# Packed attention and a routed expert layer on one core: token scores computed transposed and turned back, under a new written order

## Chip, core and metric

The kernel runs on one core of one Trainium2 chip. The metric is device time in microseconds: 563.17 us is the median of three runs of the kernel before (560.61 to 563.75). The profiled execution took 564.29 us, of which 562.5 us lie between the first and the last instruction.

## What is computed

Two attentions in a row, for 8 batches and 8 heads with 64 values each, and then a layer of eight experts in which each token goes to one.

```python
p_packed = sm_attn(p, k, v)          # 32 packed queries, 576 keys
out = sm_attn(q, p_packed, p_packed) # 576 tokens, 32 packed keys
x = out.transpose(0, 2, 1, 3).reshape(4608, 512)
e = argmax(x @ w_gate)               # one expert per token
result = gate * (relu(x @ w1[e]) @ w2[e])
```

The token scores that this case is about are q times the packed keys, in the second attention: for each token, 8 heads times 32 scores.

## The kernel before

Everything that happens up to the end of the first layer of the first phase of the experts stands in a list, `ORDER` (line 51). A token of it is one step of one generator: `S20` is the next step of the scores of batch 2, tokens 0 to 255; `c4` the next step of the scores of packed queries of batch 4, second half of the heads. `emit` (line 1051) runs one step per token, and the instructions go to their engines in that order, under `tc.manual_schedule()`. So the list is the order on every queue: TensorE (PE), VectorE (DVE), ScalarE (ACT), GpSimd (POOL), and the DMA queue of SyncE (SP). Waits between the engines are added from the tiles that instructions read and write; `need` and `acquire` only assert, while the program is built, that the list respects what they name.

The letters that matter here:

- `k`, `v`, `q` load a batch's keys with its packed queries (line 585), values (602) and tokens in two halves and a rest (610), all on SP. `cst` loads constants, the identity among them (979).
- `a` and `c` (`s1`, 630) are the scores of the packed queries: per step two matmuls with 64 stationary columns each, which stand side by side in the array, 288 columns moving (648), then a maximum on DVE and an exponential on ACT. There is one PSUM tile for them, so a `c` waits for the exponential of the `a` ahead of it.
- `r`, `u`, `l` (`tr`, `trl`, 686 and 701) turn the result by transposes, `p` (`pv`, 717) multiplies by the values, `b` (`bd`, 756) and `w` (771) prepare the packed keys (`ppT`, two heads side by side: 128 by 64) and values for the second attention.
- `S` (`s2`, 793) makes the token scores. For 256 tokens (second index 0 or 2) it has the q tile as stationary operand, 128 tokens at a time, and 64 columns of `ppT` moving: eight float32 matmuls (803). Each shows as two records in the trace. The result lies in a PSUM tile `s2` (two of them), a row per token. Then come a maximum (829), a subtraction (834), an exponential (838), a sum (842) and a product on POOL or, from batch 6 on, DVE (848). With index 4 it takes the last 64 tokens of two batches (816).
- `T` (`t2`, 854) transposes the probabilities, and `O` (`o2`, 870) multiplies them by the packed values (898, 900) and copies the result on ACT (905).
- The first 14 result tiles of `O` are held in the space of the second layer's weights (`spare`, 785) until a `W` step writes them out (787).
- `L` loads a weight block, `C` (`convert_w`, 933) splits one into two float16 parts with one ACT and one DVE instruction; `C8` to `C15` are of the second layer and write where held tiles lay.
- `R`, `E`, `F` route tokens (many small DVE steps), `G` gathers rows, `P` (538) transposes them, `M` (1212) is the first expert layer.

`tr` is a ring of four PSUM tiles that `r`, `u`, `l`, `p`, `b`, `w`, `T`, `O` and some routing steps share.

The step that changes, in the kernel before:

```python
T.matmul(
    ps[:, 256 * n + 64 * pr : 256 * n + 64 * pr + 64],
    loaded[b]["q"][i // 2][:, pr, P * n : P * n + P],
    ppTs[b % HB][:, pr, :],
    start=True,
    stop=True,
)
```

After the list come the remaining phases of the experts (from line 1238 on), whose order the builder's scheduler sets.

Of the kernel before, what the change touches and what calls it, by code (L numbers as in the profile page):

```python
# [8 lines left out]
F32 = mybir.dt.float32  # L9
# [7 lines left out]
P = 128  # L17
# [39 lines left out]
S14 S14 S12 S12 S12 T10 O00 O02 S20 r3 q2 k5 S22 v3 T10 O10 l4 S20 T12 S14 O10 k6 O10 T12 l4 l4 S20 S20 a5 c3 a5 O10
C0 O10 O02 L2 a5 O10 O12 O10 C0 O12 u4 u4 O10 O12 a5 c4 L3 w2 T14 O10 S22 c5 O12 w2 S20 O12 c5 O12 I k6 T14 O14 S22
q3 c5 r4 C1 O14 O12 C1 O14 p3 r4 p3 p3 p3 q3 S22 q3 c5 l5 O14 c5 O12 v4 O12 b3 S20 k7 l5 O00 a6 C2 u5 a6 L4 c4 b3
S32 l5 T20 S32 S30 S22 C3 O14 r5 a6 O10 S22 O12 R R R R R R R R R T20 R S32 R q4 S30 R R u5 O20 T22 a6 c6 O20 r5 S32  # L60
L5 S30 S34 T22 c6 O20 O20 C2 R O20 S34 c6 O20 O22 p4 k7 R p4 S32 S32 S30 O20 p4 C4 q4 O22 O22 p4 R O20 b4 O22 S32 w3
# [5 lines left out]
O42 S50 O40 O40 q6 E O42 E S52 E E S52 b6 T50 b6 c7 S52 E c7 E E u7 O42 L7 L8 T50 S54 S62 E l7 S62 S52 O50 S60 E O42
E S62 O40 E q7 l7 E u7 O50 S54 C6 O50 S60 O40 E O50 L9 O50 O50 l7 O40 O40 O50 O50 O40 S62 q7 O50 w6 r7 E E E E E O40
E S60 E S52 E S60 E w6 C7 E O50 E T54 W2 W3 O50 E S62 S62 T52 T54 r7 E E O54 O50 O54 S60 C7 O54 O54 p7 p7 T52 O52 E
S60 E p7 E O54 E O52 W4 W5 W6 W7 O52 O54 O52 W8 b7 p7 Z O52 W9 b7 O52 S60 q7 S62 O52 O52 O52 Z T62 O52 T62 O52 T60  # L70
S72 C6 O52 F S72 F F X F X T60 F X F F F O62 O62 F F F O62 S72 F F F F O62 W10 S72 W11 W12 W13 O62 F O62 O62 X S72
O62 F F O62 O60 F O62 L10 F S72 F F X O60 F O60 O60 S70 O62 S74 S72 O62 F X w7 T72 C8 T72 F S74 F F w7 S70 O72 O72
O72 O60 O72 F S74 O60 S74 F G0 S70 F S70 F S74 F O72 O60 F L11 S74 F X O72 S70 O60 F O60 F S70 O72 O60 O72 F O72 O72
T74 T74 S70 P0 F P0 G1 G2 P1 P1 P0 P2 F O60 P1 F F O74 P2 T70 F F F T70 F P2 O74 O74 O60 F G3 P3 P3 F O74 O72 F F
O72 F G4 O70 G5 O70 O70 C9 O70 F C10 C8 L12 F F P3 F F O70 F O70 F O70 O70 F O70 G6 G7 G8 C9 O74 F O70 F F F F O70 F
F C11 C12 O70 C11 O74 Y V0 M0 M0 M1 P4 P5 M0 P4 P5 M1 M2 M2 P4 M0 P5 M3 P6 V1 M0 C10 P6 P6 M1 M3 M4 M2 M3 M4 P7 P8
# [38 lines left out]
def packed_attention_moe(ctx, tc, qT, q1, kT, v4, v1, pT, wg, w1, w2, const, out):  # L115
# [442 lines left out]
    if True:  # L558
# [234 lines left out]
        def s2(b, i):  # L793

            need(f"b{b}", *([f"b{b - 1}"] if i == 4 else []))
            need(*([f"q{b}", f"q{b - 1}"] if i == 4 else [f"q{b}{i // 2}"]))
            acquire("s2", 2, f"s2free{b}{i}")
            ps = psq.tile([P, 512], F32, tag="s2", name="s2")
            if i < 4:
                hh = 2 * H  # L800
                for n in range(2):
                    for pr in range(NP):
                        T.matmul(  # L803
                            ps[:, 256 * n + 64 * pr : 256 * n + 64 * pr + 64],
                            loaded[b]["q"][i // 2][:, pr, P * n : P * n + P],
                            ppTs[b % HB][:, pr, :],
                            start=True,
                            stop=True,
                        )
                    if n == 0:  # L810
                        yield
            else:
                hh = H
                for pr in range(NP):
# [9 lines left out]
            done.add(f"s{b}{i}")  # L824
# [26 lines left out]
            done.add(f"e1free{b}{i}")  # L851
            es[b, i] = e
# [580 lines left out]
```

## Time and profile before

| | us |
|---|---|
| median of three runs | 563.17 (560.61 to 563.75) |
| the profiled execution | 564.29 |
| its span, first to last instruction | 562.5 |
| busy in the span: PE / DVE / ACT / POOL | 537.1 / 451.3 / 324.4 / 194.4 |
| first and last token-score matmul of 256 tokens starts (line 803) | 24.2 / 133.9 |
| first matmul of the first expert layer starts (line 1097) | 147.4 |

A busy time is the union of the records of an engine. Matmuls are pipelined, so a record is longer than the distance to the next start; where a duration decides, the distance of two starts is read. The granted clock is the share of TensorE's full 2.4 GHz.

### The profile page before, as it was taken

The page shows a single profiled execution, that of the slowest core. Times are in us where ns is not written, and L with a number is a line of the kernel's source. Part 1 is how long each engine was busy: PE and PEld are TensorE (multiplying, and loading weights), DVE is VectorE, ACT ScalarE, POOL GpSimd, SP SyncE. Part 2 cuts the span into 40 slices and gives each one's busy share as a digit, 9 for nine tenths or more (in the row PEclk, how much of TensorE's full clock was granted, in tenths as well). Part 3 has the DMA queues.
Part 4 walks back from the last instruction along what each step waited for, and adds up shares of the span by engine and source line. Part 5 has one row for each costly group of instructions (what it writes and reads, how often), then busy time and mean ns, then how long its engine had stood idle before and what let it go on. Part 6 is the DMA issues. An engine that isn't in the chain of part 4 may idle for free.

```text
span 562.5 us, 13282 instructions
## 1 busy us (share of the span) xinstructions
PE 537.1 (95%) x4055; PEld 322.8 (57%) x4055; DVE 451.3 (80%) x928; ACT 324.4 (58%) x663; POOL 194.4 (35%) x277
## 2 busy tenths in 40 slices
PE   4999999998898999999999999999999999999994
PEld 2687687876565456544644655565456456545541
DVE  1366788989998989998999797777449998997962
ACT  2355866566786877734853762366868438736600
POOL 3122333225661102400210266477823302302374
PEclk9999999998999999999999999999999999999998
DMA  8899866999897956984996599378869968975883
GB/s 315 333 399 386 323 247 195 356 325 314 285 223 181 273 185 158 282 196 172 267 244 235 151 170 342 109 169 188 298 252 255 267 212 174 293 255 143 184 239 125
DMA packets 118615, 136.71 MB, mean 243 GB/s; under 512 B 82895, under 2 KB 95311, under 8 KB 116624
## 3 DMA queue, kind: packets, MB, share of 16 engines
q1 hardware_dynamic: 112624, 116.65, 71.8%
q0 software_dynamic: 5920, 19.14, 10.6%
q8 instruction: 41, 0.67, 0.5%
q14 instruction: 30, 0.25, 0.1%
HBM read 97.49 MB, written 19.14 MB: 207 GB/s over the span
## 4 chain that ended last, share of the span: by engine, by line
PE 80%; DVE 10%; ACT 3%; issue 3%; DMA 2%; POOL 0%; POOLq 0%; SPq 0%; DVEq 0%; ACTq 0%
PE py L1156 30%; PE psa L1097 19%; PE psa L1100 9%; PE s L803 5%; PE x L898 5%; PE s L648 4%; PE psx L544 2%; PE pv L739 2%; DVE y L1165 1%; DVE w1r L188 1%; PE t L864 1%; PE tr L695 1%; DVE u L1106 1%; DMA h<-hs 1%; ACT a L663 1%
## 5 line engine op out<-in xcount | busy, mean ns | idle before, releaser
L1097 PE MATMUL psa<-w1r,x 128*128 (+1 forms) x656 | 194.4, 380 | 1.6 <-DVE w1r L188 1.1
L1156 PE MATMUL py<-w2r,h 128*128 (+1 forms) x984 | 195.6, 379 | 0.0
L1100 PE MATMUL psa<-w1r,x 128*128 (+1 forms) x656 | 161.6, 273 | 0.0
L1156 PEld LDWEIGHTS <-h 128*128 128x128 f16 (+1 forms) x984 | 87.5, 100 | 101.6 <-issue 2.9
L1123 POOL TENSOR_TENSOR hs<-u,hs 128x256 f16<-128x256 f32 x74 | 64.7, 876 | 221.2 <-DVE hs L1120 203.7
L1097 PEld LDWEIGHTS <-x 128*128 128x128 f16 (+1 forms) x656 | 58.8, 100 | 68.0 <-issue 2.4
L1165 DVE SCALAR_TENSOR_TENSOR y<-py,gpl,y 128x512 f32<-128x512 f32 x111 | 79.8, 739 | 13.6 <-PE py L1156 13.5
L1104 ACT ACTIVATE u<-psa 128x256 f32<-128x256 f32 x148 | 52.6, 376 | 42.2 <-PE psa L1100 38.2
L188 DVE SCALAR_TENSOR_TENSOR w1r<-stage,w1r 128x1024 f16<-128x1024 f32 x48 | 58.8, 1225 | 11.7 <-ACT w1r L187 11.7
L188 DVE SCALAR_TENSOR_TENSOR w2r<-stage,w2r 128x1024 f16<-128x1024 f32 x48 | 59.8, 1246 | 10.2 <-ACT w2r L187 10.1
L187 ACT ACTIVATE w1r<-stage 128x1024 f16<-128x1024 f32 x48 | 49.2, 1048 | 27.9 <-DMA stage<-w 27.9
L1100 PEld LDWEIGHTS <-x 128*128 128x128 f16 (+1 forms) x656 | 58.9, 100 | 8.6 <-issue 2.4
L1106 DVE SCALAR_TENSOR_TENSOR u<-psa,u 128x256 f32<-128x256 f32 x148 | 57.5, 412 | 7.6 <-ACT u L1104 7.3
L187 ACT ACTIVATE w2r<-stage 128x1024 f16<-128x1024 f32 x48 | 50.2, 1045 | 1.1 <-DMA stage<-w 1.1
L1127 DVE SCALAR_TENSOR_TENSOR hs<-u,hs 128x256 f16<-128x256 f32 x74 | 39.8, 539 | 6.1 <-ACT hs L1125 5.8
L1176 POOL DMA_INDIRECT out_rows<-y,sca x37 | 38.6, 1044 | 12.8 <-issue 8.6
L1125 ACT ACTIVATE hs<-u 128x256 f16<-128x256 f32 x74 | 30.4, 412 | 21.2 <-DVE u L1106 18.4
L1118 ACT ACTIVATE u<-u 128x256 f32<-128x256 f32 x74 | 30.6, 414 | 19.0 <-DVE u L1106 19.0
L547 ACT ACTIVATE x<-psx,xup 128x512 f16<-128x512 f32 x37 | 25.0, 686 | 26.5 <-PE psx L544 26.4
L898 PE MATMUL x<-bd,a2T 128*128 128x264 f32 x128 | 37.3, 418 | 0.0
L549 DVE SCALAR_TENSOR_TENSOR x<-psx,xup,x 128x512 f16<-128x512 f32 x37 | 27.4, 746 | 5.9 <-ACT x L547 5.8
L803 PEld LDWEIGHTS s<-ppT,q 128*128 128x128 f32 x256 | 30.8, 192 | 2.0 <-issue 0.9
(180 smaller groups left out, 633.5 us busy)
## 6 DMA issues: line engine op xcount, KB each, us to landing
stage<-w SPq DMA_DIRECT2D x112, 512.0 KB, 4.6
v<-v SPq DMA_DIRECT2D x8, 1024.0 KB, 10.3
q<-qT SPq DMA_DIRECT2D x16, 512.0 KB, 8.8
k<-kT SPq DMA_DIRECT2D x7, 1152.0 KB, 6.3
xd<-x SPq DMA_DIRECT2D x22, 256.0 KB, 5.2
xd<-w2r SPq DMA_DIRECT2D x14, 256.0 KB, 4.6
h<-hs SPq DMA_TRANSPOSE x76, 4.6
k<-kT SPq DMA_DIRECT2D x2, 576.0 KB, 5.1
```

The source lines that it names most:

```text
L187: A.activation(hi, src, AF.Copy, scale=SW)
L188: V.scalar_tensor_tensor(lo, src, SW, hi, op0=ALU.mult, op1=ALU.subtract)
L803: T.matmul(ps[:, 256 * n + 64 * pr : 256 * n + 64 * pr + 64], loaded[b]["q"][i // 2][:, pr, P * n : P * n + P], ppTs[b % HB][:, pr, :], st ...
L898: T.matmul(ps, aT[:, 2 * n + g, :], bds[b % HB][:, g, :], start=True, stop=True)
L1097: T.matmul(ps[c], x[:, 0, k, c], w, start=(k == 0), stop=False, **kw)
L1100: last["T"] = T.matmul(ps[c, 0:FC], x[:, 1, k, c], w, start=False, stop=(k == 3), **kw)
L1104: A.activation(u, ps[:, FC:], AF.Copy, scale=SH)
L1106: V.scalar_tensor_tensor(u, ps[:, 0:FC], SH, u, op0=ALU.mult, op1=ALU.add)
L1123: last["G"] = G.tensor_tensor(hs[:, 1], u, hs[:, 0], op=ALU.subtract)
L1127: last["V"] = V.scalar_tensor_tensor(hs[:, 1], u, 0.0, hs[:, 0], op0=ALU.max, op1=ALU.subtract)
L1156: last["T"] = T.matmul(ps[c], h[:, hp, f, c], w, start=(n == 0), stop=(n == 5), **kw)
L1165: last["V"] = V.scalar_tensor_tensor(y, ps, at(gpls, j), y, op0=ALU.mult, op1=ALU.add)
```

## The change

1. `s2` for 256 tokens: the packed keys are now the stationary operand (64 columns, two side by side at partitions 0 and 64) and 256 tokens of q move. That is two steps of two matmuls, into a tile of the `tr` ring. ACT copies this tile (128 by 512) to a new SBUF tile `sT` (two of them), and four PE transposes turn it back into the `s2` tile. What follows is as before. There are two more steps per unit, and 16 such units.
2. `convert_w` asserts, for a second-layer block, only the held tiles that lie in its own stretch of the space, and not all 14.
3. `ORDER` is written anew: 1074 tokens where there were 1042.

```diff
 ORDER = """
-k0 k0 a0 a0 a0 a0 cst c0 k1 c0 c0 cst c0 r0 r0 k1 v0 c0 l0 c0 k2 a1 l0 k2 a1 u0 q0 a1 l0 a1 c1 c1 u0 p0 c1 p0 p0 r1
-c1 q0 r1 l1 wgs p0 b0 l1 c1 a2 b0 a2 S02 a2 k3 S02 a2 c2 S02 c2 S00 l1 c2 c2 S02 u1 r2 S00 v1 S00 S00 k3 a3 u1 c1
...
-O62 F O62 O62 O60 F O62 L10 F S72 F F X O60 F O60 O60 S70 O62 S74 S72 O62 F X w7 T72 C8 T72 F S74 F F w7 S70 O72 O72
...
+q0 k0 k0 a0 a0 a0 a0 k1 cst v0 cst q0 k1 wgs c0 wgs c0 c0 c0 c0 r0 u0 l0 a1 u0 r0 k2 a1 l0 k2 v1 c0 l0 p0 a1 a1 p0
+c1 p0 c1 b0 c1 I b0 p0 S02 S00 S00 c1 S02 k3 c1 S00 a2 a2 a2 S00 w0 S02 S00 q0 q1 q1 q1 a2 r1 w0 r1 l1 l1 S00 u1 l1
...
+O62 S72 O62 W13 F G0 F C8 C9 O62 O60 O62 S70 T74 T70 F T74 F O62 S72 F X T70 O74 O74 F S72 O74 O74 F O70 F O70 X O74
+F L10 F F O70 F O62 F T72 F O62 X F O70 T72 F O72 P0 F O72 L11 O72 F O74 O70 F F F F G1 F F G2 F G3 O70 F F F P0 P0
...
             if i < 4:
                 hh = 2 * H
-                for n in range(2):
-                    for pr in range(NP):
+                acquire("tr", 4, f"st{b}{i}")
+                pt = pst.tile([P, 2, 256], F32, tag="tr", name="sT")
+                for g in range(2):
+                    for j in range(2):
                         T.matmul(
-                            ps[:, 256 * n + 64 * pr : 256 * n + 64 * pr + 64],
-                            loaded[b]["q"][i // 2][:, pr, P * n : P * n + P],
-                            ppTs[b % HB][:, pr, :],
+                            pt[64 * j : 64 * j + 64, g, :],
+                            ppTs[b % HB][:, 2 * g + j, :],
+                            loaded[b]["q"][i // 2][:, 2 * g + j, :],
                             start=True,
                             stop=True,
                         )
-                    if n == 0:
+                    if g == 0:
                         yield
+                done.add(f"s{b}{i}")
+                yield
+                acquire("sT", 2, f"sT{b}{i}")
+                sT = wk.tile([P, 2, 256], F32, tag="sT", name="sT")
+                A.copy(sT, pt)
+                done.add(f"st{b}{i}")
+                yield
+                acquire("s2", 2, f"s2free{b}{i}")
+                ps = psq.tile([P, 512], F32, tag="s2", name="s2")
+                for n in range(2):
+                    for g in range(2):
+                        T.transpose(ps[:, 256 * n + P * g : 256 * n + P * g + P], sT[:, g, P * n : P * n + P], ident)
+                done.add(f"sT{b}{i}")
...
-            need(f"stage{w}", *([f"x{t}" for t in range(14)] if w[0] else []))
+            need(f"stage{w}", *([f"x{t}" for t in range(ND) if t < (w[2] + 1) * 4096 / 2112 and t + 1 > w[2] * 4096 / 2112] if w[0] else []))
```

## Rows read from the trace of the kernel before

**Rows 1.** The page's busy times and its chain by engine.
```profile
PE 537.1 (95%) x4055; PEld 322.8 (57%) x4055; DVE 451.3 (80%) x928; ACT 324.4 (58%) x663; POOL 194.4 (35%) x277
...
PE 80%; DVE 10%; ACT 3%; issue 3%; DMA 2%; POOL 0%; POOLq 0%; SPq 0%; DVEq 0%; ACTq 0%
```

**Rows 2.** Busy time by stretch: length, PE, PEld, DVE, ACT, POOL, clock, DMA share, GB/s.
```profile
24.00:115.00 91.00, 90.36 (x1152) 71.72 (x1149) 69.12 (x181) 56.50 (x134) 27.41 (x52) 1.00 0.86 319
115.00:148.00 33.00, 28.36 (x301) 22.20 (x301) 30.55 (x111) 20.45 (x47) 15.62 (x19) 0.95 0.94 302
148.00:182.00 34.00, 31.23 (x217) 20.83 (x216) 30.90 (x73) 25.77 (x58) 15.71 (x17) 1.00 0.87 227
182.00:262.00 80.00, 78.93 (x438) 40.70 (x437) 77.37 (x154) 49.87 (x86) 11.69 (x13) 1.00 0.83 221
262.00:562.00 300.00, 292.43 (x1820) 158.99 (x1818) 238.61 (x401) 164.98 (x327) 116.96 (x148) 0.99 0.80 216
```

**Rows 3.** Chain that ended last, in order of time: start us, us, what.
```profile
36.02 2.63 PE s L803 x24
...
39.65 0.84 PE s L803 x8
...
40.48 0.44 PE t L864 x4
...
52.14 1.73 PE s L803 x16
...
74.72 0.49 PE s L648 x4
```

**Rows 4.** Timeline of PE, 36 to 60 us: start us, us, engine, line, operation.
```profile
39.03 0.61 PE L898 MATMUL x<-bd,a2T 128*128 128x264 f32 x2
39.48 1.00 PE L803 MATMUL s<-ppT,q 128*128 128x64 f32 x8
...
48.47 1.06 PE L898 MATMUL x<-bd,a2T 128*128 128x264 f32 x4
49.36 0.60 PE L695 MATMUL tr<-cst,a 128*128 128x128 f32 x4
...
54.75 0.61 PE L898 MATMUL x<-bd,a2T 128*128 128x264 f32 x2
55.29 1.19 PE L648 MATMUL s<-k,pb 128*64 128x288 f32 x8
56.41 1.16 PE L898 MATMUL x<-bd,a2T 128*128 128x264 f32 x4
57.41 0.60 PE L695 MATMUL tr<-cst,a 128*128 128x128 f32 x4
```

**Rows 5.** Groups of ACT, 24 to 115 us: count, busy us, mean ns, idle before.
```profile
L698 ACT COPY aT<-tr 128x512 f32<-128x512 f32 x12 | 7.1, 590 | 1.8 <-PE tr L695 1.8
```

**Rows 6.** DMA rate in 40 slices of the stretch 0 to 60 us.
```profile
GB/s 0 121 350 406 443 412 418 389 275 399 328 287 313 95 326 427 404 382 403 388 423 392 369 388 376 411 435 421 397 421 426 332 270 424 380 405 399 409 423 373
```

**Rows 7.** Timeline of all engines, 0 to 24 us.
```profile
1.17 0.42 SPq L592 DMA_DIRECT2D k<-kT  x1
...
5.18 2.19 PE L648 MATMUL s<-k,pb 128*64 128x288 f32 x8 [5.18 <-DMA k<-kT]
...
11.20 1.12 PE L695 MATMUL tr<-cst,a 128*128 128x128 f32 x4
...
17.31 2.19 PE L648 MATMUL s<-k,pb 128*64 128x288 f32 x8 [0.68 <-ACT a L663]
...
19.43 1.08 PE L739 MATMUL pv<-v,aT 128*32 128x64 f32 x32
```

**Rows 8.** Timeline of PE, 110 to 150 us.
```profile
126.55 3.01 PE L898 MATMUL x<-bd,a2T 128*128 128x264 f32 x12
...
132.69 0.63 PE L864 MATMUL t<-cst,e 128*128 128x128 f32 x4 [1.50 <-DVE n L335]
...
134.05 4.62 PE L898 MATMUL x<-bd,a2T 128*128 128x264 f32 x12
```

**Rows 9.** Busy time by engine in stretches of 5 us (columns as in rows 2).
```profile
135.00:140.00 5.00, 4.76 (x21) 3.72 (x19) 4.23 (x18) 3.90 (x11) 2.22 (x3) 0.75 0.86 304
```

More of the change, by code (lines that the diff above doesn't have):

```diff
@@ L57 @@
[L57 to L61, printed above, removed]
@@ L67 @@
[L67 to L71, printed above, removed]
@@ L72 @@
[L72 to L76, printed above, removed]
@@ new lines @@
+c1 p0 c1 b0 c1 I b0 p0 S02 S00 S00 c1 S02 k3 c1 S00 a2 a2 a2 S00 w0 S02 S00 q0 q1 q1 q1 a2 r1 w0 r1 l1 l1 S00 u1 l1
+c2 S00 u1 c2 c2 c1 k3 S02 S00 c2 k4 p1 p1 u2 a3 u2 S02 p1 a3 S00 b1 T00 b1 p1 S02 w1 k4 S10 a3 a3 S10 c3 S02 q2 T00
+c3 c3 O00 c2 w1 S02 S12 S10 O00 S12 c3 O00 r2 O00 O00 S10 v2 q2 S14 S10 S12 L0 l2 l2 r2 l2 u3 u3 S14 l3 S14 l3 S02
+k5 T02 T02 a4 v3 O00 S10 S10 S14 O02 S10 a4 S14 S10 S12 l3 O02 O00 p2 S12 a4 a4 O00 O02 T10 p2 c4 O02 c4 c2 p2 T10
+O00 O02 I p2 S14 S12 S12 O00 b2 b2 O02 O10 O10 O10 c3 k5 c4 O10 L1 O02 O10 c4 S22 S22 r3 S22 S20 S20 S22 S12 l4 O02
@@ new lines @@
+l4 S20 S22 S20 r3 a5 a5 l4 S22 c4 a5 O10 S12 O02 C0 T12 O10 r4 O10 k6 S20 a5 c5 S20 c5 c5 T12 O10 O12 S20 v4 O02 T14
+r4 O12 k6 T14 S20 O12 w2 w2 O10 q2 O12 q3 q3 S22 O12 c3 O12 O14 O14 O12 u4 c5 q3 O14 p3 p3 u4 O14 C1 S20 O12 a6 S22
+C0 p3 p3 l5 a6 l5 a6 O12 b3 b3 O14 O12 R R T20 C1 R l5 R T20 R R S30 S22 S30 q4 c5 c5 q4 S34 S30 R O20 a6 S34 L2 L3
+L4 S34 T22 O20 c4 S30 O20 T22 O20 S34 R R S30 q4 c6 O20 R O20 c6 R S32 O20 S30 R k7 p4 R S32 S34 S30 C2 S32 S30 C3
+C4 p4 R c6 S32 O22 S34 O22 O22 S30 R O22 p4 b4 p4 C3 R b4 O20 O22 O20 S32 O22 v5 O22 L5 T30 S32 T30 c6 w3 O22 S42
@@ new lines @@
+O22 S42 T34 T34 S42 R S32 w3 O30 O30 O30 O30 O30 O30 O30 C4 S40 k7 R O30 S40 O34 R S40 C2 O30 R O22 r5 R S42 S40 S32
+O30 O34 O34 S42 r5 l6 u5 O34 S42 S32 u5 O34 S42 S40 p5 L6 O30 l6 l6 T32 S40 O20 S42 T32 C5 q5 O34 p5 O32 S40 O32 p5
+q5 a7 O32 O32 C6 p5 w4 C5 q5 a7 b5 O32 q6 b5 O32 a7 O32 S42 O32 w4 c6 W0 O32 O32 S50 O32 S40 S52 C6 S50 T42 O32 a7 E
+E E v6 S54 S54 E T42 S50 E c7 S54 S52 E c7 O42 E S54 L7 S50 S40 c7 S52 O42 O42 E E r6 S50 E c7 q6 u6 S52 O42 E r6 c6
+q6 S50 E T40 E S50 E u6 p6 E p6 T40 O40 E O40 S52 O40 E O40 O42 S54 O42 E p6 W1 E p6 E b6 r7 w5 b6 O42 S62 S62 S50
@@ new lines @@
+r7 O42 w5 E O42 S62 O40 u7 u7 E l7 S54 S52 O42 T54 S62 E S60 l7 S52 S62 c7 S60 O40 E S52 l7 T54 E S50 S60 O40 S62
+O40 O40 E O54 S60 O40 S60 E v7 O40 E c7 T50 S62 O42 S52 E E T50 E O54 O42 q7 O54 p7 O40 S60 p7 T52 E p7 O54 E O50
+S60 C7 q7 W2 E O50 O50 O50 O54 O54 T52 p7 E E b7 C7 E O52 b7 O52 S70 O50 S60 W3 O52 S70 O52 W4 S70 O50 w6 O50 Z O50
+E O50 q7 O52 O50 E S62 E E E L8 E E E O52 w6 S60 S70 E E S74 O52 S62 O52 E O52 E E O50 S74 Z E E T60 W5 W6 O50 S72
+S74 E S70 O52 T60 L9 T62 O52 O52 S74 O60 E T62 O60 O60 E W7 F F F F O60 S74 O60 F S74 F S72 F S72 F F O62 X F S70
@@ new lines @@
+S70 F S72 X F F F O62 F S70 F w7 O62 S72 O62 F W8 W9 F w7 O60 O60 W10 O60 F O60 W11 W12 O60 S72 F X O60 F F X O62
+O62 S72 O62 W13 F G0 F C8 C9 O62 O60 O62 S70 T74 T70 F T74 F O62 S72 F X T70 O74 O74 F S72 O74 O74 F O70 F O70 X O74
+F L10 F F O70 F O62 F T72 F O62 X F O70 T72 F O72 P0 F O72 L11 O72 F O74 O70 F F F F G1 F F G2 F G3 O70 F F F P0 P0
+O72 F O70 P1 O70 F F F P1 O70 F O72 F O72 F O70 G4 F F F P2 P2 P1 O72 O70 O72 C10 O72 F G5 O70 C9 F P2 F P3 P3 G6 P3
+O72 O72 G7 C11 C8 O72 F F L12 Y V0 M0 M0 M1 M1 P4 M0 P5 P4 P5 P4 M0 M2 M2 P6 P5 M2 P6 M1 P6 M2 M3 M3 M1 G8 P7 P8 P7
@@ new lines @@
+C10 M4 P7 P8 G9 P8 V1 P9 M3 M2 C12 P9 M3 M1 M4 G10 M0 P10 G11 G12 G13 G14 P9 P10 P10 M5 M0 P11 P11 M2 M4 P11 C11 M5
+M3 M6 P12 P13 M6 M5 P13 M4 M6 P13 M7 M6 M6 L13 M4 M5 G15 P12 M5 P12 M7 M8 M8 M9 P14 M8 M7 P15 C13 C13 M4 M9 G16 M7
+M1 M8 M8 G17 M10 P14 P14 M9 P15 M10 M11 L14 M7 M3 M6 C12 M9 G18 M8 L15 C14 P15 M11 C15 M11 M12 M9 M10 C15 M12 M13
+P16 P17 M12 M10 M11 P17 P16 P16 M5 M12 M10 M12 P17 M13 M14 M14 M14 M15 M11 P18 P18 M12 M13 M13 P18 M13 M7 M14 C14
+M10 M15 M16 M16 M17 M17 M18 M15 M17 M15 M9 M16 M18 M14 M18 M11 M15 M16 M17 M17 M13 M18 M16 M18 L16 M16 M14 M15 M18
@@ L82 @@
+M17 L17 L18 L19 M18
 """
@@ L796, in s2 @@
             need(*([f"q{b}", f"q{b - 1}"] if i == 4 else [f"q{b}{i // 2}"]))
-            acquire("s2", 2, f"s2free{b}{i}")
-            ps = psq.tile([P, 512], F32, tag="s2", name="s2")
             if i < 4:
                 hh = 2 * H
-                for n in range(2):
-                    for pr in range(NP):
+                acquire("tr", 4, f"st{b}{i}")
+                pt = pst.tile([P, 2, 256], F32, tag="tr", name="sT")
+                for g in range(2):
+                    for j in range(2):
                         T.matmul(
-                            ps[:, 256 * n + 64 * pr : 256 * n + 64 * pr + 64],
-                            loaded[b]["q"][i // 2][:, pr, P * n : P * n + P],
-                            ppTs[b % HB][:, pr, :],
+                            pt[64 * j : 64 * j + 64, g, :],
+                            ppTs[b % HB][:, 2 * g + j, :],
+                            loaded[b]["q"][i // 2][:, 2 * g + j, :],
                             start=True,
@@ L809, in s2 @@
                         )
-                    if n == 0:
+                    if g == 0:
                         yield
+                done.add(f"s{b}{i}")
[11 more added lines that the diff above has]
+                done.add(f"sT{b}{i}")
             else:
                 hh = H
+                acquire("s2", 2, f"s2free{b}{i}")
+                ps = psq.tile([P, 512], F32, tag="s2", name="s2")
                 for pr in range(NP):
@@ L823, in s2 @@
                 ps = ps[:, 0:256]
-            done.add(f"s{b}{i}")
+                done.add(f"s{b}{i}")
             yield
```

13 lines of the change are left out of this document (removed).

## The prediction, made before the changed kernel ran

> **What bounds the kernel now.** The page comes first: PE is busy for 95% of the span, DVE for 80%, ACT for 58%, and the chain that ended last lies on PE for 80% and on ACT for 3% [rows 1]. That is an average, so the busy times by stretch come next [rows 2]. From 24 to 115 us PE is busy 90.36 of 91 us while DVE has 69.12 and ACT 56.50: here the attention is a matter of PE's work, and what PE need not do is gained. From 115 to 182 us PE has 59.6 of 67 us and DVE 61.45: routing, conversions and softmax share DVE, and PE waits now and then. From 182 us on PE is busy 371.4 of 380 us, so a start that is earlier by some time stays earlier by it.
>
> **Token scores, PE's part.** Before, a unit of 256 tokens is 8 float32 matmuls, 16 records. In the chain 24 records take 2.63 us and 8 take 0.84, so one costs 1.79/16 = 0.112 us and a unit 1.79 us; a unit that stands alone took 1.73 [rows 3]. The trace does not show the new form. The nearest rows are the packed queries' scores at line 648: they have the same shape, two 64-column matmuls side by side, with 288 columns instead of 256. Four of their records take 0.49 us [rows 3]; at 256 columns that is 0.436, and for the two steps 0.87. The four transposes that turn the tile back are like those at line 864, 0.44 us for four [rows 3]. New unit: 1.31 us. Over 16 units 16 x (1.79 - 1.31) = 7.7 us less.
>
> Against this stands the change of shape between full and 64-column matmuls. Two records before a line-648 group take 0.54 us (54.75 to 55.29) where two elsewhere take 0.45 (39.03 to 39.48): 0.09. The group itself takes 1.12 (55.29 to 56.41) where two times 0.49 would be 0.98: 0.14. The four records behind it take 1.00 (56.41 to 57.41) where four elsewhere take 0.89 (48.47 to 49.36): 0.11 [rows 3, 4]. One excursion into 64 columns and back thus costs 0.23 to 0.34 us; I take 0.30, nearer the upper end, because what follows is mostly line 898 or transposes. I counted the shapes along both lists, without the routing matmuls: 71 changes before, 107 after, so 18 more excursions, 18 x 0.30 = 5.4 us. PE's net gain is 7.7 - 5.4 = **2.3 us** (1.6 at 0.34, 3.6 at 0.23, 7.7 if excursions were free).
>
> The rows show 0.436 us for a pair of 64-column matmuls and 0.3 us for going there and back. The Trainium skill, TensorEngine Tiling, Performance Considerations, advises just this swap where the moving side has 64 columns or fewer, and its Overview names a speedup of up to 2x; by that alone the sum would be 16 x 0.895 = 14.3 us less for the scores and 7.0 more for transposes, 7.3 us gained. The same page, Key Properties, says that changing the tiling mode drains the TensorE, without a price; the trace agrees, and its price takes most of that.
>
> **ACT and PSUM.** 16 copies of 128 by 512 from PSUM are added, at 0.590 us [rows 5] 9.4 us. 14 of the units lay before 115 us, so ACT goes there from 56.50 to 64.8 us of 91 (71%). I cost them at nothing: ACT's idle 34 us hide them. If that cover is gone, PE pays, since its queue is in order: four transposes wait for the copy, the next users of the four-tile `tr` ring wait for the tile that the copy frees, and whatever is queued behind waits with them. DVE's maximum comes later by the copy, but between a unit's second matmul step and its transposes the list puts 1 to 12 other PE steps. DVE's and POOL's work per unit is the same.
>
> **Conversions.** The condition that is loosened is an assertion at build time; the waits follow from the tiles. In the new list W13 stands ahead of C8 as it did before, so the looser condition admits nothing that is used: nothing gained, nothing lost.
>
> **The start.** The new list sends the first half of q0 (512 KB) ahead of p0 and both parts of k0 on SP; p1, k1, v0 and the constants queue behind too. At the 350 to 443 GB/s of the slices from 3 to 7.5 us [rows 6], 0.52 MB take 1.3 us, and the first matmul, which waits for k0 until 5.18 us, comes as much later. The constants now stand behind about 3.0 MB, by the same rate some 10 us, still ahead of the first transposes at 11.20 (+1.3) [rows 7]. The half of the q load would have come later anyway. In return p0's matmuls stand ahead of c1's. Before, c1 waited 0.68 us for an exponential at 17.31 and p0 started behind it at 19.43 [rows 7]; afterwards p0 fills that gap and its DVE step runs beside c1. I put the return at 1.0 us, an estimate from the 0.68 and a short wait behind p0. Net **+0.3 us**, between -1 and +1.5.
>
> **The new order behind 115 us.** PE waits 1.50 us for DVE before T72's transposes at 132.69, and soon after, from 134.05, twelve records of line 898 take 4.62 us where twelve took 3.01 at 126.55 [rows 8]. The granted clock of 135 to 140 us is 0.75 [rows 9]: part of it is at 1.2 instead of 2.4 GHz. That costs 1.6 us. In the old list 4 steps lie between S72's last and T72's first, in the new one 16, so I expect that wait, and the slow stretch with it, to go: **-1.6 us** (0 if another wait takes its place, +1.6 if there are two). DVE's work in this stretch is unchanged, so DVE is late next, and more than its 5.55 idle us [rows 2] cannot come out. The phases behind the list have the same instructions; their scheduling may shift by a microsecond either way.
>
> **Sum.** -2.3 + 0.3 - 1.6 = -3.6 us. From the profiled execution's 564.29 us that is 560.7; this execution is 1.1 us above the median of 563.17, so I forecast 559.6 against the median. A measurement of this kernel tells about 0.5% (2.8 us) from no change.
>
> **Rivals.**
> 1. ACT's copy becomes the wait, and the kernel is slower. Place: the transposes of a unit, and the `tr` ring behind it, from 24 to 135 us. For it: 71% of ACT's time with everything in order, and weight conversions that can stand ahead of a copy. Against it: ACT has only 3% of the chain now. Price: 0.59 us for each exposed copy. It decides from about 8 of the 16 units on, which eat the 2.0 us of the first two terms and 2.8 more. With 12 exposed it is 563.2 - 2.0 + 7.1 = 568.3 us. Chance 0.21. The Trainium skill, TensorEngine Tiling, PSUM Bottleneck, warns of this: tiling speeds up TensorE, not the evacuation of PSUM, and the copy may become the bottleneck; the rows so far don't bear it out, as ACT waits for PE's transposes (1.8 us ahead of line 698) [rows 5] and not the reverse.
> 2. DVE takes the gain back. PE reaches 115 us 2 us earlier, but DVE, busy 61.45 of 67 us, sets when the first expert layer can run, and new waits stand where T72's stood. For it: those two numbers. Against it: DVE has 22 us idle before 115 us and can start its share earlier. Price: the gain; about 563 us. Chance 0.32.
> 3. The excursions cost less than the rows say, since the two steps of a unit often stand back to back with `s1` steps or another unit: with all of 7.7 us and the slow stretch gone it would be 563.2 - 7.7 + 0.3 - 1.6 = 554.2. This is the far end of the forecast's side, not a case of its own.
>
> **How the numbers follow.** Faster (forecast and its far end) 0.47, absorbed 0.32, ACT-bound 0.21; these are also the chances of faster, same and slower. The forecast's own range is 553 to 561. The range of 8 in 10 goes down to 553, the far end with the start at its best, and up to 567, short of rival 1's centre: about 0.1 is left above and 0.1 below.
>
> **What would show it.** Right: token-score pairs of records about 0.22 us apart; 64 more transposes at 0.11 us; 16 ACT copies near 0.59 us; PE's stretch from its first score matmul to the last `O` of batch 5 shorter by some 2 us, busy above 97%; no stretch of granted clock at half between 130 and 140 us; the first line-1097 matmul near 144 us instead of 147.4. Wrong: PE idle ended by the new ACT copy for more than 3 us in total (rival 1); the first line-1097 matmul still near 147 with DVE steps as the releasers (rival 2); the first matmul later than 6.8 us, or the slow matmuls of the start lasting longer.

## The result, and the profile after

The changed kernel took 567.66 us (median of 22 runs, 563.25 to 571.85), the kernel before beside it 563.45 us: a ratio of 1.0077, 95% interval 1.0053 to 1.0101. It is slower by 0.8%, where 0.6% faster had been forecast, and lies just above the range. The experiments below were measured in five groups (a to d, e to h, i to l, m to o, p to r), each beside the kernel before; in the second, third and fourth every kernel, that one too, took about 9 us more (the mean granted clock of the kernel before was 0.985 to 0.986 there, against 0.993 to 0.994 in the first and the last), so between groups ratios are compared, and times only within one.

The page of the changed kernel, its busy times and its chain by engine. Its profiled execution took 568.04 us, 566.1 of them between the first and the last instruction.

```profile
PE 531.6 (94%) x3991; PEld 305.2 (54%) x3991; DVE 451.6 (80%) x928; ACT 331.8 (59%) x679; POOL 189.9 (34%) x277
...
PE 83%; DVE 7%; DMA 4%; ACT 3%; issue 1%; POOL 1%; SPq 0%; POOLq 0%; ACTq 0%; DVEq 0%
```

PE does 5.5 us less than in [rows 1], ACT 7.4 more, DVE the same, and yet the span is 3.6 us longer. So PE waits more. The stretches say where (columns as in [rows 2]); the last row answers to [rows 9].

```profile
24.00:115.00 91.00, 90.83 (x1186) 60.57 (x1183) 68.70 (x175) 65.70 (x154) 27.22 (x55) 1.00 0.84 312
115.00:148.00 33.00, 24.83 (x206) 17.03 (x205) 29.54 (x117) 20.28 (x46) 12.23 (x18) 1.00 0.95 320
148.00:182.00 34.00, 29.58 (x196) 19.55 (x196) 29.80 (x68) 24.36 (x54) 15.62 (x17) 1.00 0.94 209
182.00:262.00 80.00, 78.56 (x445) 40.57 (x444) 76.20 (x154) 50.36 (x90) 12.13 (x13) 1.00 0.81 221
...
135.00:140.00 5.00, 3.73 (x22) 2.17 (x20) 4.69 (x23) 3.49 (x9) 3.82 (x5) 1.00 0.69 202
```

From 24 to 115 us PE is as full as before. From 115 to 148 us it is busy for 24.83 us instead of 28.36. A stretch of fixed ends cannot say whether that is work saved or work not yet done, so the table is cut again at the first matmul of the first expert layer, which is at 147.38 us before and at 149.00 after. First the kernel before, then the changed one:

```profile
0.00:24.00 24.00, 15.75 (x138) 8.31 (x138) 4.73 (x10) 6.78 (x14) 7.01 (x30) 1.00 0.86 312
...
115.00:147.38 32.38, 27.74 (x297) 21.83 (x297) 29.96 (x108) 19.84 (x46) 15.01 (x19) 0.95 0.93 301
sum 147.38, PE 133.85 PEld 101.86 DVE 103.82 ACT 83.11 POOL 49.43; mean PE 44.62 PEld 33.95 DVE 34.61 ACT 27.70 POOL 16.48
```

```profile
0.00:24.00 24.00, 12.60 (x131) 6.65 (x133) 4.83 (x12) 6.09 (x13) 5.75 (x27) 1.00 0.85 315
...
115.00:149.00 34.00, 24.83 (x206) 17.03 (x205) 30.51 (x121) 21.28 (x48) 13.23 (x18) 1.00 0.95 320
sum 149.00, PE 128.25 PEld 84.25 DVE 104.03 ACT 93.07 POOL 46.20; mean PE 42.75 PEld 28.08 DVE 34.68 ACT 31.02 POOL 15.40
```

This is the account of the change. Up to the expert layer PE's busy time fell from 133.85 to 128.25 us, by 5.6. Its idle time rose from 13.5 (147.38 - 133.85) to 20.75 us, by 7.2: 3.15 more in the first 24 us (11.4 against 8.25), 0.5 less up to 115, and 4.5 more behind (34.00 - 24.83 = 9.17 against 4.64). The difference, 1.6 us, is how much later the expert layer starts; its first layer adds 0.9 (the second layer's first matmul comes at 184.95 instead of 182.44), and the rest to 3.6 us comes in the phases behind.

Not all of the 5.6 us is work saved, since part of both sums ran at half speed. From the first matmul to 21.50 us before, and to 19.77 us after, matmuls take about twice as long as later: eight records of the packed queries' scores last 2.19 us there (at 17.31 us before, 17.29 after) and 1.19 us behind it (at 23.09 and 21.20). The clock column reads 1.00 in that stretch only because the trace's records of the clock begin where it ends. A second stretch, which the clock column does show, lies behind 134 us in the kernel before. The rows are of the kernel before, of the changed kernel, and of run b below (old form, new list):

```profile
5.18:21.50 16.32, 13.25 (x121) 6.82 (x121) 3.47 (x6) 4.53 (x11) 2.49 (x6) 1.00 0.91 332
134.10:137.50 3.40, 3.40 (x9) 2.65 (x9) 2.63 (x10) 1.72 (x5) 1.88 (x2) 0.51 0.88 312
```

```profile
8.22:19.77 11.55, 9.15 (x49) 4.36 (x53) 2.11 (x5) 3.00 (x7) 2.33 (x5) 1.00 1.01 393
```

```profile
6.83:18.09 11.26, 8.87 (x37) 4.07 (x41) 1.87 (x4) 3.00 (x7) 2.32 (x5) 1.00 1.03 413
144.40:147.80 3.40, 2.91 (x34) 2.52 (x35) 1.74 (x5) 1.07 (x2) 2.79 (x3) 0.50 1.01 378
```

Counting busy time at half speed as half gives an estimate of PE's work at full speed up to the first expert matmul. The last line of the table counts, along the matmuls of the trace, how often their shape changes between full and narrower ones.

| | before | old form, new list (b) | changed kernel |
|---|---|---|---|
| PE busy, us | 133.85 | 133.82 | 128.25 |
| of it at half speed, us | 16.65 | 11.78 | 9.15 |
| work at full speed, us | 125.5 | 127.9 | 123.7 |
| changes of shape | 71 | 87 | 107 |

The other traces agree: 125.5 to 126.3 us with old form and list (e, k, n, p), 127.9 and 128.2 with the old form in the new list (f, l), 123.0 to 124.1 with the new form in it (c, d, g to j, m, o). So the change saves PE 1.8 us of work: the list alone adds 2.4 us, along with 16 changes of shape, and the form takes 4.2 off. The other 3.8 of the 5.6 us are clock: 2.05 at the start and 1.7 behind 134 us.

Little of that clock can be put down to the change. At the start it differs between executions of one kernel: in the traces of d and i (one kernel, the changed one with an early load put back), the half speed ends at 18.93 and at 12.38 us, and the same transposes run first at half and then at full speed:

```profile
13.15 1.12 PE L696 MATMUL tr<-cst,a 128*128 128x128 f32 x4 [0.68 <-ACT a L664]
```

```profile
13.16 0.66 PE L696 MATMUL tr<-cst,a 128*128 128x128 f32 x4 [0.68 <-ACT a L664]
```

Behind 115 us the changed kernel's profiled execution has no stretch at half clock, but its mean granted clock, 0.997, is reached by only 4 of its 22 executions. Their mean is 0.993, that of the kernel before (17 executions of the first group) is 0.993 too, and d's trace has such a stretch:

```profile
138.40:145.20 6.80, 6.14 (x45) 5.03 (x46) 4.63 (x18) 2.51 (x5) 5.05 (x6) 0.50 1.01 360
```

PE's timeline in the first 24 us (answers to [rows 7]), and from 130 to 150 us (to [rows 8]):

```profile
8.22 2.19 PE L650 MATMUL s<-k,pb 128*64 128x288 f32 x8 [8.22 <-DMA k<-kT]
...
132.47 0.46 PE L1024 MATMUL xmax<-dg,onef 128*128 128x128 f32 x2 [1.82 <-DVE dg L1022]
...
138.74 0.71 PE L915 MATMUL x<-bd,a2T 128*128 128x264 f32 x2 [0.73 <-ACT a2T L884]
141.07 0.66 PE L546 MATMUL psx<-cst,y 128*128 128x128 f32 x4 [1.62 <-DMA y<-xd,gat]
...
144.63 0.63 PE L546 MATMUL psx<-cst,y 128*128 128x128 f32 x4 [1.25 <-DMA y<-xd,gat]
...
149.00 0.38 PE L1114 MATMUL psa<-w1r,x 128*128 x1 [1.52 <-issue]
```

The first matmul waits for k0 until 8.22 us instead of 5.18. The 1.50 us ahead of T72 are gone, as forecast, and so is the slow stretch behind it in this execution (135 to 140 us: clock 1.00). In their place stand the scale's matmul behind DVE's `dg`, two transposes of gathered rows behind the gather, and 1.52 us ahead of the expert layer.

The form itself: ACT's group of the new copy from 24 to 115 us (answers to [rows 5]), and PE's timeline from 50 to 54 us (to [rows 4]).

```profile
L818 ACT COPY sT<-sT 128x512 f32<-128x512 f32 x14 | 8.1, 588 | 4.0 <-PE sT L805 4.0
```

```profile
50.31 1.08 PE L805 MATMUL sT<-q,ppT 128*64 128x256 f32 x8
51.33 0.66 PE L697 MATMUL tr<-cst,a 128*128 128x128 f32 x4
...
52.93 0.66 PE L825 MATMUL s<-cst,sT 128*128 128x128 f32 x4
53.42 0.27 PE L710 MATMUL trl<-cst,a 128*128 128x128 f32 x1
```

A unit's two steps take 1.02 us from start to start, with the change of shape in it, and its transposes 0.49: 1.51 us where the old form took 1.79.

### The profile page after: what moved, and what is told of

Read it like the earlier page. It is cut to its first block, busy times and chain, and to the rows that moved or that the text cites. A ratio compares the mean times of both kernels' runs of the same rounds, so it can differ in the third digit from the quotient of the medians.

```text
span 566.1 us, 13186 instructions
## 1 busy us (share of the span) xinstructions
PE 531.6 (94%) x3991; PEld 305.2 (54%) x3991; DVE 451.6 (80%) x928; ACT 331.8 (59%) x679; POOL 189.9 (34%) x277
## 4 chain that ended last, share of the span: by engine, by line
PE 83%; DVE 7%; DMA 4%; ACT 3%; issue 1%; POOL 1%; SPq 0%; POOLq 0%; ACTq 0%; DVEq 0%
PE py L1173 31%; PE psa L1114 21%; PE psa L1117 10%; PE x L915 4%; PE s L650 4%; PE sT L805 3%; PE psx L546 2%; PE tr L697 1%; PE pv L741 1%; DMA out_rows<-y,sca 1%; DMA y<-xd,gat 1%; PE s L825 1%; DMA k<-kT 1%; PE t L881 1%; DVE x L551 1%
## 5 line engine op out<-in xcount | busy, mean ns | idle before, releaser
L915 PE MATMUL x<-bd,a2T 128*128 128x264 f32 x128 | 38.6, 409 | 1.4 <-ACT a2T L884 1.3
L650 PE MATMUL s<-k,pb 128*64 128x288 f32 x128 | 22.9, 472 | 10.3 <-DMA k<-kT 8.2
```

The source lines that it names most:

```text
L650: T.matmul(ps[64 * j : 64 * j + 64, i, 0:288], p_s[:, 2 * g + j, :], k_s[:, 2 * g + j, 288 * i : 288 * i + 288], start=True, stop=True,)
L915: T.matmul(ps, aT[:, 2 * n + g, :], bds[b % HB][:, g, :], start=True, stop=True)
```

## The experiments

### The form and the list apart

**New form, old list (a_form_old_order).** The copy is written right behind the unit's matmuls and the transposes right ahead of its maximum; seven steps are moved forward so that each ring has room.

```diff
-a2 S02 a2 k3 S02 a2 c2 S02 c2
+a2 S02 a2 k3 S02 S02 a2 c2 S02 S02 c2
```

> The new form of the token scores in the old written order: the copy stands right behind a unit's matmuls, the four transposes right ahead of its maximum, and seven steps are pulled ahead where a PSUM tile must be free; the start, the W steps and X stay as before. Theory 1 (the new order costs, the form gains): 560 to 562 us, 2 to 4 below the kernel before; first gather near 132 us, first expert matmul 145 to 147 us. Theory 2 (the form costs, through ACT's copies and PE's waits for them): 566 us or more, PE idle behind the copy or behind a2T for over 3 us.

Measured: 583.13 us, ratio 1.0332 (1.0284 to 1.0379). Its stretch from 24 to 115 us, and then its waits there (engine and line, what it waited for: us in total, times, longest):

```profile
24.00:115.00 91.00, 79.67 (x910) 50.61 (x906) 53.57 (x128) 52.40 (x122) 21.43 (x43) 0.94 0.75 279
```

```profile
DVE m L845 <- PE s L824: 20.5, 9, 4.8
...
ACT sT L817 <- PE sT L804: 10.0, 9, 2.2
...
PE s L824 <- ACT sT L817: 1.4, 2, 0.7
```

PE is idle for 11.3 us of a stretch in which it had 0.64. With nothing written between a unit's matmuls, copy, transposes and maximum, each stands at the head of its queue and waits: DVE for the transposes, ACT for the matmuls, and what is queued behind them. PE itself waited 1.4 us for the copy, but 4.7 us for ACT's exponentials of the packed queries and 2.6 for the turned probabilities, which are queued on ACT too. Part of the loss is clock (0.94 in the stretch). This written order does not carry the form; other places for its steps in the old list were not tried.

**Old form, new list (b_oldform_new_order).** The matmul steps stand where the new list has the second step and the transposes.

```diff
-b0 p0 S02 S00 S00 c1 S02 k3 c1 S00 a2
+b0 p0 S00 c1 S02 k3 c1 a2
```

> The old form of the token scores in the new written order: the two matmul steps stand where the new form has its second matmul step and its transposes; S14, S52 and S72 start later where an s2 tile must be free. Theory 1: the order's cost without the form's gain, 569 to 573 us, above the changed kernel's 567.7. Theory 2: near the kernel before, 562 to 565 us.

Measured: 570.31 us, ratio 1.0101 (1.0054 to 1.0148). Its stretch from 115 us to its first expert matmul at 152.5, and PE's longest waits there:

```profile
115.00:152.50 37.50, 29.13 (x306) 22.66 (x304) 33.80 (x131) 21.85 (x50) 14.28 (x19) 0.95 0.96 310
sum 152.50, PE 133.82 PEld 100.53 DVE 104.79 ACT 85.96 POOL 47.62; mean PE 44.61 PEld 33.51 DVE 34.93 ACT 28.65 POOL 15.87
```

```profile
PE psx L544 <- DMA y<-xd,gat: 2.6, 1, 2.6
PE x L898 <- ACT a2T L867: 1.5, 3, 0.7
PE psa L1097 <- issue: 1.5, 1, 1.5
```

PE is busy as long as in the kernel before (133.82 against 133.85), but less of that is at half speed, so its work is 2.4 us more; and its idle time behind 115 us is 8.37 us against 4.64. So the 3.7 us of idle time come from the list, whatever the form: the waits for the gather, for the turned probabilities and ahead of the expert layer are the changed kernel's.

**Both forms under the new list with the early load put back (d_q0_back, f_oldform_q0_back; once more as i_q0_back_again and l_oldform_again, side by side).** d and i are the changed kernel, f and l the kernel of b, each with this edit:

```diff
-q0 k0 k0 a0 a0 a0 a0 k1 cst v0 cst q0 k1
+k0 k0 a0 a0 a0 a0 k1 cst v0 cst q0 q0 k1
```

> The changed kernel with the first half of q0 loaded right ahead of its second half, behind k0, k1, the constants and v0, as in the kernel before. The first matmul should come near 5.2 us instead of 8.2. If the start is on the path: 1 to 3 us below the changed kernel (565 to 566.5). If the later stages wait for DVE anyway, or the values then land later: within 1 us of 567.7.

> The scores as before the change, in the new list, with the first half of q0 loaded right ahead of its second half (as in the run d_q0_back). Against d_q0_back it tells what the transposed form is worth under one and the same list. Theory A (the form's gain on PE reaches the end): this is 3 to 6 us slower than d_q0_back, a ratio to the kernel before of 1.006 to 1.012. Theory B (DVE takes the gain back behind 95 us): the eighth product with the values (batch 7) starts 5 to 8 us later than in d_q0_back, but the first gather and the first matmul of the expert layer come within 1.5 us of that run's, and the ratio is 1.000 to 1.004.

> The kernel of d_q0_back again, as the control of this job, since the job before ran on a chip whose times of the kernel before are 9 us longer. Both theories: ratio to the kernel before 0.998 to 1.004, as it was (1.0008).

> The kernel of f_oldform_q0_back again, beside the control on one chip: scores in the old form, list and loads as in the control. Theory D or V (PE is ahead with the new form, but what follows is bound elsewhere): within 2.5 us of the control. Rival (the form's gain on PE reaches the end under this list): 4 to 6 us slower than the control, as the ratios of the two jobs say (1.0095 against 1.0008).

Measured: new form 1.0008 (0.9978 to 1.0039) and 1.0049 (1.0015 to 1.0084), old form 1.0095 (1.0074 to 1.0115) and 1.0089 (1.0055 to 1.0122). Busy times up to the first expert matmul, of i and then of l:

```profile
sum 152.27, PE 129.81 PEld 85.45 DVE 104.42 ACT 93.03 POOL 50.80; mean PE 43.27 PEld 28.48 DVE 34.81 ACT 31.01 POOL 16.93
```

```profile
sum 157.20, PE 135.44 PEld 101.94 DVE 105.11 ACT 85.19 POOL 51.15; mean PE 45.15 PEld 33.98 DVE 35.04 ACT 28.40 POOL 17.05
```

Under one list PE is busy 5.6 us less with the new form (135.44 - 129.81), 4.4 of them work at full speed by the count above, and the expert layer starts 4.9 us earlier. By the ratios the form is worth 0.4% (i and l, whose intervals overlap; side by side their medians are 575.20 and 579.05 us) to 0.9% (d and f, of different groups), 2 to 5 us. The list without it costs 0.9%.

### The start

**The early load alone, in the kernel before (e_old_q0_first).**

```diff
-k0 k0 a0 a0 a0 a0 cst c0
+q0 k0 k0 a0 a0 a0 a0 cst c0
...
-k2 a1 u0 q0 a1 l0
+k2 a1 u0 a1 l0
```

> The kernel before, with one step of its list moved: the first half of q0 is loaded ahead of k0. It prices the start alone. Theory (the start costs what it showed): the first matmul comes at about 8 us instead of 5.2, and since PE is busy from then on to 115 us, 2 to 3 us of it are left at the end: ratio to the kernel before 1.004 to 1.006 (the later half of the load no longer competes, which may give 0.5 us back). Rival (the delay is swallowed, because DVE sets the pace from about 95 us on and has idle time ahead of that): first matmul at 8 us, but the first matmul of the expert layer within 0.5 us of 147.4 and a ratio of 1.000 to 1.002.

Measured: first matmul at 8.40 us, ratio 1.0026 (0.9993 to 1.0059): some 1.5 us, not told from nothing. The delay itself differs between traces: with the load ahead the first matmul came at 6.83 (b), 8.22 (the changed kernel), 8.40 (e) and 8.80 us (c), without it at 5.18 to 5.62. Taken out of the changed kernel the same step brings it from 1.0077 to 1.0008 (d) and 1.0049 (i), 1.6 to 3.9 us, and the first matmul back to 5.34 us:

```profile
5.34 2.19 PE L649 MATMUL s<-k,pb 128*64 128x288 f32 x8 [5.34 <-DMA k<-kT]
```

### What holds up the expert layer under the new list

**Writes of held tiles (c_w_early, j_writes_in_gap, k_old_writes_in_gap).** c: the changed kernel with W3 to W13 one after every three other steps behind W2. j is d, and k the kernel before, with W0 to W8 moved to where the trace shows the DMA engines empty (0.15 of the time from 74 to 86 us after). The edit of j:

```diff
-O22 v5 O22 L5 T30
+O22 v5 O22 W0 W1 W2 W3 W4 W5 W6 W7 W8 L5 T30
```

> The changed kernel with the writes W3 to W13 of the held tiles issued earlier, one after every three other steps behind W2; all else in the changed kernel's order. If the late writes hold up the first gather (135.4 us against 131.9 before): gather near 132 us, first expert matmul 1 to 2 us earlier than 149.0, total 565 to 566.5 us. If DVE's backlog or the scale step X is what ends last there: first expert matmul still near 149 us, total 567 to 568.5.

> d_q0_back with the writes W0 to W8 of held tiles put ahead of the load of the sixth weight block (L5). In d_q0_back the DMA engines stand empty for some 9 us between 73 and 83 us, and are busy all the time from 106 to 132 us, where those writes lie: nine of 256 KB are 2.36 MB, by 330 GB/s 7 us. Theory D (from 106 us on DMA is the bound: the gather waits for the writes that end last): the gap is filled, the last write of a held tile is issued at 122 to 127 us instead of 128.5, the first gather starts at 126 to 130 us instead of 133.0, and the time falls by 2 to 5 us against the control. Theory V (DVE's order is the bound: routing steps stand behind softmax steps): the gap is filled all the same, but the first gather stays within 1 us of 133.0 and the time within 1 us of the control's.

> The kernel before with the same edit: W0 to W8 right behind the load v5, ahead of the 8 us from 82 to 88 and around 76 us in which DMA is empty. Theory D: first gather 2 to 5 us ahead of 131.9, ratio 0.991 to 0.997. Theory V: first gather within 1 us of 131.9, ratio 0.998 to 1.002.

Measured: c 1.015 (1.0101 to 1.0198), j 1.0061 (1.0028 to 1.0094), k 0.9981 (0.9949 to 1.0013). Both expectations of c fell. There the writes stand ahead of the last load of tokens on SP, and PE waits for it:

```profile
PE s L832 <- DMA r<-q: 4.8, 1, 4.8
```

In k the first gather comes at 128.7 us (before: 131.9), in j at 131.8 against 131.5 in its control. But k's 3.2 us are not the writes' doing. Its first token score already starts at 21.4 us (before: 24.2), ahead of the first W, since in its trace the half speed of the start ends at 13.0 us and not at 21.50; only some 0.3 us more are gained behind that.

```profile
L803 PE MATMUL s<-ppT,q x256: 219/275/323, 21.4 to 130.7; 128*128 128x64 f32 x128
```

j had left W13 where the new list has it, with one step between it and the first gather (the old list: 50 steps), and the control's trace of POOL shows that gather waiting for a write:

```profile
131.50 1.25 POOL L529 DMA_INDIRECT y<-xd,gat  x1 [4.39 <-DMA xd<-x]
```

The traces of d (the same kernel) and of the changed kernel put the wait at this place down to a routing step on DVE instead (3.79 and 3.86 us). So j did not test what it was to test, whether the last write or the routing holds the gather stays open, and k gained nothing that can be measured.

**All of the gather's conditions early (m_all_early from d, n_old_all_early from the kernel before), and o_all_early_p_behind, which is m with P0 to P3 behind the last O.**

```diff
-S54 L7 S50
+S54 L7 W9 W10 W11 W12 W13 S50
...
-E W7 F F F F O60 S74
+E F F G0 F F X O60 S74
```

> d_q0_back with all 14 writes of held tiles early (W0 to W8 ahead of L5, W9 to W13 behind L7), the first four gathers 3, 20, 40 and 60 steps behind the end of the first routing stage (E), and the scale (X) 12 steps earlier. In j_writes_in_gap W9 to W13 and the gather had kept their places, and the gather its time. Theory D2 (the last held writes and the gather's place on POOL set the gather's start): first gather at 121 to 126 us, first transposes of gathered rows 3 to 6 us earlier, and a ratio to the kernel before of 0.993 to 0.999. Theory O (the O steps of batch 7, which stand behind those transposes on PE and behind three x tiles on ACT, set the start of the expert layer): the first gather comes early too, but the last O matmul stays at 146 to 150 us and the ratio at 1.000 to 1.006.

> The kernel before with the same moves: W0 to W8 behind v5, W9 to W13 behind L6, the first four gathers earlier, X 8 steps earlier. k_old_writes_in_gap, with W0 to W8 alone, had its first gather at 128.7 us and a ratio of 0.998. Theory D2: first gather at 121 to 126 us, ratio 0.988 to 0.995. Theory O (PE's own work bounds the old form: it is idle for 4.6 us of the 33 before the expert layer): first gather early, first matmul of the expert layer not ahead of 143 us, ratio 0.994 to 0.999.

> m_all_early with the steps of P0 to P3 behind the last O step. Theory D2: with the gathered rows there in time this order costs nothing or 1 us. Theory O: the last O matmul ends at 136 to 143 us, the first matmul of the expert layer comes 2 to 5 us earlier than in m_all_early, ratio 0.990 to 0.998. If the writes of x tiles are slow beside the gathers, as in the run g_p_behind_o, the O steps wait for them and it is slower than m_all_early.

Measured: m 1.0073 (1.0037 to 1.0109), n 1.0012 (0.9975 to 1.0048), o 1.0171 (1.0123 to 1.0218). n's first gather on POOL, and then its PE:

```profile
124.77 1.25 POOL L528 DMA_INDIRECT y<-xd,gat  x1 [0.17 <-DMA r<-q]
```

```profile
139.42 0.41 PE L864 MATMUL t<-cst,e 128*128 128x128 f32 x2
139.67 1.04 PE L544 MATMUL psx<-cst,y 128*128 128x128 f32 x8
...
150.01 0.38 PE L1097 MATMUL psa<-w1r,x 128*128 x1 [1.01 <-issue]
```

The gather starts 7 us earlier than in the kernel before, and its rows are transposed at 139.67 all the same, since PE has work until then: in the old list the gather is not what PE waits for. In m the five writes behind L7 hold up the load of tokens (PE waits 3.8 us for it, and is busy for 87.03 us instead of 90.14 from 24 to 115 us), so m prices that and not the gather. Neither m nor n came out in the range of either theory; o, with the transposes behind the last O as in g below, is slower still.

**Routing first (h_route_first), and the transposes of gathered rows behind the last O (g_p_behind_o), both from d.** h writes E and F 20 steps earlier, X 15, W 8, G 6; g takes P0 to P3 out from between the O steps:

```diff
-F O72 P0 F O72 L11 O72 F O74 O70 F F F F G1 F F G2 F G3 O70 F F F P0 P0 O72
+F O72 F O72 L11 O72 F O74 O70 F F F F G1 F F G2 F G3 O70 F F F O72
```

> d_q0_back with the routing steps (E, F) written 20 places earlier, the scale of x (X) 15, the writes of held tiles 8, the gathers 6; the rest keeps its order. Theory (DVE is back to back from 95 us on, and its order decides when the gather can start): the expert index of the first stage is ready at 119 to 121 us instead of 122.8, the first gather starts at 129 to 131 us instead of 133.0, the first matmul of the expert layer at 144 to 146 us instead of 147.7, and the time is 1.5 to 3.5 us below that of d_q0_back (ratio 0.995 to 0.999). Rival (DVE's total decides, whatever the order): the gather comes earlier, but the last O matmuls later, and the first matmul of the expert layer stays within 0.7 us of 147.7 at a ratio of 1.000 to 1.003.

> d_q0_back with all steps of P0 to P3 (the transposes of gathered rows) written behind the last O step. There the last O matmuls stood behind transposes that waited 4.3 us for the gather. Theory (these queued O matmuls hold up what follows): the last O matmul ends 2 to 4 us earlier than 146.3, but the transposes come later, so the first matmul of the expert layer moves by -1 to +1 us, and the ratio to the kernel before is 0.998 to 1.002. Rival (the gather is all that counts): the last O matmul ends near 142 and the expert layer's first matmul stays within 0.3 us of 147.7, time unchanged.

Measured: h 1.0127 (1.0106 to 1.0148), g 1.0123 (1.0105 to 1.0142); both expectations fell. In h the first gather came at 138.3 us, later and not earlier. A routing step that is written earlier waits 1.2 us for its own input at the head of DVE's queue (`mx`, for POOL's `lg`; d has no such wait), and the token scores come later (the last one ends at 129.0 us against 124.3 in g); that this is the whole of the delay is not shown. In g the last O matmul did end at 142.9 us, but ACT's copies then waited up to 8.8 us between two of them, and the expert layer started at 159.4. Behind 115 us and up to the expert layer PE was busy at half clock for 5.5 us in g and 12.1 in h (3.4 in the kernel before, 6.1 in d), so part of the loss, of h's above all, is clock.

**More x tiles (p_old_x5: five in the kernel before; q_q0_back_x4: four in d, and one sT tile; r_x4_p_behind: q with the move of g).**

```diff
-                        x = wk.tile([P, 2, 264], F32, tag="x", name="x", bufs=3)
+                        x = wk.tile([P, 2, 264], F32, tag="x", name="x", bufs=5)
```

> The kernel before with five x tiles for the copies of O results instead of three (two size constants; list unchanged). In n_old_all_early the first gather came 7 us early and the expert layer did not, so the gather's start is not what sets it. Theory R (the three x tiles: ACT's copies of the last O results wait until a write to DRAM has landed, which takes long beside the gathers): the last ACT copy of an O result comes 2 to 5 us earlier than in the kernel before, the first matmul of the expert layer too, ratio 0.990 to 0.997. Rival (PE and the place of the transposes of gathered rows on its queue set it): ratio 0.998 to 1.002.

> d_q0_back with four x tiles instead of three, and one sT tile instead of two to make room (one step of S42 moved seven places forward for it). Theory R: the wait of ACT's copy for a landed write between 137 and 146 us shrinks by 2 us or more, ratio 0.995 to 1.001, below d_q0_back on such a chip (1.0008, 1.0049). Rival: 1.002 to 1.008; a single sT tile may cost up to 1 us of it.

> q_q0_back_x4 with P0 to P3 behind the last O step, as in g_p_behind_o (1.0123). Theory R: with a fourth tile the O steps run through, so it is much better than g_p_behind_o: ratio 0.997 to 1.004. Rival: 1.008 to 1.016, as g_p_behind_o, so the transposes' place is what costs.

Measured: p 0.999 (0.9954 to 1.0026), q 1.0063 (1.0031 to 1.0095), r 1.0128 (1.0077 to 1.0179). The x tiles are not what holds the kernel before (first expert matmul at 147.5 us, as it was), and a fourth one does not mend g's order.

No version here is faster than the kernel before by more than the measurement can tell; the nearest, k, has 0.9981. Of the list's 0.9% (5 us, f and l) some 2 us can be PE's added work, with 16 more changes of shape. What remains open is which of the waits behind 115 us carries the rest, and how much of it is clock (on average 0.982 in f and l, 0.985 to 0.986 in the kernel before beside them): taken singly, none of the waits that were moved gave it back.

## Why the prediction was wrong

- **PE's net gain, forecast 2.3 us: right, in size and mechanism.** PE's work at full speed fell by 1.8 us, within the 1.6 to 3.6 of the prediction, and the trace has the 71 and 107 changes of shape that were counted. What the prediction did not separate: 16 of the 36 added changes come with the list alone, where they cost 2.4 us (0.30 for one excursion, as assumed); the form brings the other 20 and gains 4.2 to 4.4 us under one list. A unit of 1.51 us, with its change of shape, gives nearly the same: 16 x (1.79 - 1.51) = 4.5 us. Rival 3, excursions that cost next to nothing, is not borne out.
- **ACT's copies cost nothing: right under the new list.** They took 588 ns (590 in [rows 5]), ACT rose to 65.70 us of 91 (forecast 64.8), and the list of PE's waits is empty from 24 to 115 us and has no wait for the new copy up to 149 us. Rival 1 came near in another place: with the old list (a) the copy and the transposes hold up DVE and ACT, at 3.3%. The Trainium skill, TensorEngine Tiling, PSUM Bottleneck, says that after a 4x speedup of TensorE the copy out of PSUM may become the bottleneck. The changed kernel's trace does not show that, and in a's PE waited 1.4 us for the copy itself.
- **The conversions:** no run tried the looser condition by itself, and none shows anything against its zero.
- **The start, forecast +0.3 (between -1 and +1.5): failed in size.** The first matmul came 3.0 us later, not 1.3, and so beyond the 6.8 us that the prediction named as a sign of being wrong: half of q0 (0.52 MB) in 3.0 us is 170 GB/s, half the rate taken from later slices [rows 6]. (In b the same load cost 1.65 us.) The return of 1.0 us did not show: PE was idle 3.15 us more in the first 24. That 2.05 us came back because the half speed ended sooner was not in the prediction, and was luck of the execution. What of the delay reaches the end is 1.5 to 3.9 us by e, i and d.
- **The new order behind 115 us, forecast -1.6: this is the step that failed.** The wait ahead of T72 went, as the step says; the slow stretch went from the profiled execution, but not on average, by the granted clocks. The step looked only at the wait that the new list removes, and bounded the rest by two waits of that size (+1.6). The list also writes the last W right ahead of the first gather, the scale's steps later (the first X at place 720 of 1074, before 669 of 1042), and an O right behind its T. Measured, PE's idle time there rose by 4.5 us; with the old form under the same list (b) by 3.7, so it is the list's and not the form's.
- **Rival 2** named the place (behind 115 us) and one of the engines (DVE's `dg`, 1.82 us), and stopped at the gain; it did not allow that the list could take more than that. The chance of slower, 0.21, hung on ACT alone.

The sum as measured in the two profiled executions, up to the expert layer: -1.8 (PE's work) + 3.15 - 2.05 (start: idle time, and half speed that ended sooner) - 0.5 (24 to 115 us) + 4.5 - 1.7 (behind 115 us: idle time, and the slow stretch) = +1.6 us, where the prediction had -3.6.

## What to carry to other kernels

Price a new order by the idle time of the bounding engine up to one common event, before and after, and look in it for each wait's conditions (what must have landed, and how many steps lie between), not only for the wait that the change is to remove. Before two busy times are compared, take the clock out of them: here 3.8 of 5.6 us were clock, and two traces of one kernel differed by 6.5 us in how long the start ran at half speed. A form that adds hand-overs between engines needs other work written between them: the same form gained 0.4 to 0.9% in one list and lost 3.3% in the other. Test an order and a form apart, by putting each into the other's kernel; that took two runs here and showed that the loss is the list's, which the traces of before and after alone could not.

## What was not expected

A load of 0.5 MB ahead of the first one needed put off the first matmul by 3.0 us in the changed kernel's trace, and by 1.65 to 3.6 us in all traces that have it. The DMA engines were nearly empty from 74 to 86 us (0.15 busy) and full from 115 to 148 (0.95), while loads stood on SP's queue behind a weight load and a write that still waited. Writes put into a like gap of the kernel before (k) moved the gather by some 0.3 us, and the time by nothing that can be measured. Where gathers and writes of results run together, in i's trace but not in d's of the same kernel, ACT's copy of an O result waited up to 7.3 us for an event that the trace puts down to no engine of this core; by the code it may be the write of the x tile's former content, which was not tried apart (more x tiles were only run where this wait did not show). The row is from i's waits from 128 to 156 us:

```profile
ACT x L921 <- remote: 7.3, 1, 7.3
```
